# Two accumulator tiles of the last token group, moved to a pool of their own on the other side of SBUF

## The chip, the cores and the metric

The kernel runs on one core of one Trainium2 chip. Times are device microseconds (us) of one execution; of several runs the median is taken. An engine's name stands for its row in the profile: PE is the matrix engine, PEld its weight loads, DVE the vector engine, ACT the scalar engine, POOL the GpSimd engine (here it only issues DMAs), SP the engine that issues the other DMAs.

## The reference

Sigmoid attention for 8 batches of 12 heads, then a bilinear feed-forward net over all 3584 tokens:

```python
scores = scale * np.matmul(q, k.transpose(0, 1, 3, 2)) - np.log(S)   # S = 448, head size 64
attn = 1.0 / (1.0 + np.exp(-scores))
x = np.matmul(attn, v)          # heads side by side: 3584 tokens x 768
a = x @ w1                      # 768 -> 1024
b = x @ w2
h = a * b @ w3                  # 1024 -> 1024
out = h @ w_out                 # 1024 -> 768
```

All in float32; the weights come in as 64-bit words and are decoded on the chip.

## The kernel before

**Precision.** Each float32 operand is split into a high and a low part; a product is three matmuls (high by high, high by low, low by high).

**Stages.** Four token groups, each of two batches, go through attention (scores, sigmoid, times V) and then through `up(g)`, which computes `a`, `b` and their elementwise product. The two products of a 2 by 2 block split are made with seven block products instead of eight (L342 gives the operands, `POPS` and `NEEDS` the order of side work). A block product is 9 matmuls of 448 columns. The eight feature blocks `fc` take seven products each, so `up(g)` has 56 products. The last group, g = 3, is the "ending": nothing of attention is left to run beside it. After it come the product of `w3` with `w_out` (L852) and the final product with the activations (L984).

**Order.** From L577 on, the order of the instructions on all five engines is the order in which the code emits them. `take(stream, n)` advances a generator by n steps; nine steps of `up` are one block product. A load of `w` for the product five places ahead is issued on SP (L440, from L517) as each product begins; six `w` buffers go round.

**The last group's order** (L428 to L430) begins with `(fc, k)` = (0,0) (0,2) (1,0) (0,1) (1,2) (0,3) (0,4) (0,5) (0,6), and then (1,1) (2,0) (1,3) (1,4) (1,5) (1,6) (2,1) (2,2) (2,3) and so on. So `fc` 0 and 1 are interleaved, and two tiles of `fc` 1 are needed beside those of `fc` 0: `p_1` (the kept copy of product (1,0), read by the additions of (1,1) and (1,3)) and `c11_1` (the kept copy of (1,2), read by the multiplication of (1,6), L503). `kept` (L494 to L497) takes these two from the pool `p2`, all other kept tiles from `pm`.

**Pools in SBUF.** `pm` stands on the left side, open to the end of `phase_x` (L786). On the right side stand `pa` and `pf` (attention), and above them first `p1`, from step k = 46 on `p2` (the words `raw` and `f` of the last weights to be decoded, and the two tiles). After nine products of the ending the code does this:

```python
    take(filler, 9 * KH * 3 - 9)      # L740: the first nine products of the ending
    take(rest, 10 ** 6)
    phase_2.close()                   # p2
    phase_a.close()                   # pa, pf
    p3 = phase_w.enter_context(tc.tile_pool(name="p3", bufs=2, side="right"))   # L747
    load_wo(0); load_wo(1)            # L774, POOL: wof <- wo_dram
    load_w3(0, nc.gpsimd); load_w3(1, nc.gpsimd)
    for jc in range(NF):
        take(filler, 42 if jc else 54)                                          # L779
        split(woh[:, jc], wol[:, jc], wof.pop(jc), nc.scalar.copy, nc.vector)   # ACT L79, DVE L80
        load_wo(jc + 2)
```

`p3` takes the room that `pa`, `pf` and `p2` leave; its first instructions wait for the last use of what lay there. So at the point where POOL reaches the four loads of L774 to L777, six products of `fc` 1 and 2 that still use `p_1` and `c11_1` are not yet done; they are emitted by `take(filler, 54)`. The first split (ACT L79 into `woh`, DVE L80 into `wol`) stands, on ACT and on DVE, behind the instructions of these six products and ahead of those of (2,1).

`leave` (L502) multiplies into the output block and stores it to `g_dram` on POOL (L504).

Of the kernel before, what the change touches and what calls it, by code (L numbers as in the profile page):

```python
# [11 lines left out]
F32 = mybir.dt.float32  # L12
# [13 lines left out]
def sigmoid_attention_bilinear_ffn(  # L26
# [17 lines left out]
    B, H, D, S = qT.shape  # L44
    DM, DF = w1.shape[0], w1.shape[1] // 2
    NT = B * S
    P = 128
# [12 lines left out]
    def share_upper(kind):  # L60

        if upper:
            if upper[-1][0] == kind:
                return
            upper.pop()[1].close()
        if kind:
            stack = ExitStack()
            upper.append(
                (kind, stack, stack.enter_context(tc.tile_pool(name=kind, bufs=1, space=PSUM)))
            )  # L70
# [50 lines left out]
    phase_x = ExitStack()  # L121
# [90 lines left out]
    def attention(sp):  # L212
        a = pa.tile([P, 2, S], F32, name="a", bufs=4)
        sigmoid(a, sp)
        return a
# [220 lines left out]
    def load_weights(i):  # L436
        if i < len(stream):
            n = stream[i]
            ring[n] = pm.tile([P, 2, KH, P], F32R, name="w", bufs=RING)
            nc.sync.dma_start(out=ring[n].bitcast(F32), in_=w_dram[n % (NF * 7)])  # L440
# [33 lines left out]
    def up(g):  # L474

        at = {b: slice(b * S, (b + 1) * S) for b in (2 * g, 2 * g + 1)}
        ending = g == NG - 1
        parts = {fc: {} for fc in range(NF)}
        banks = {fc: {} for fc in range(NF)}

        def chain(fc, bank):
            if ending:
                tag = ("sp" if fc == 1 else "up0", "up1", "av", "av")[bank]
            else:
                tag = ("up0", "up1")[(len(banks[fc]) + fc) % 2]
            if tag == "sp":
                acc = ps.tile([P, 2, 512], F32, name="sp", bufs=2)[:, 0, :S]
            elif tag == "av":
                acc = ps.tile([P, 512], F32, name="up", tag=tag, bufs=2)[:, :S]
            else:  # L490
                acc = upper[-1][2].tile([P, 512], F32, name="up", tag=tag)[:, :S]
            banks[fc][bank] = acc

        def kept(name, fc=0):  # L494
            if ending and fc == 1:
                return p2[0].tile([P, S], F32, name=f"{name}_1", bufs=1)
            return pm.tile([P, S], F32, name=name, bufs=1)  # L497

        def add(out, a, b):
            nc.vector.tensor_tensor(out=out, in0=a, in1=b, op=ALU.add)  # L500

        def leave(fc, b, a, c, out):  # L502
            nc.vector.tensor_tensor(out=out, in0=a, in1=c, op=ALU.mult)  # L503
            nc.gpsimd.dma_start(out=g_dram[fc, :, at[b]], in_=out)  # L504

        first = stream[g * NF * 7:g * NF * 7 + 7]
        for done, n in enumerate(stream[g * NF * 7:(g + 1) * NF * 7]):
            share_upper("products")
            k = n % 7
            fc = n // 7 % NF  # L510
            name = PRODUCTS[k]
            part = parts[fc]
            if g == 0:
                while n not in ring:
                    next(weights)
            else:
                load_weights(place[n] + RING - 1)  # L517
            w = ring.pop(n)
            bank, start, stop = ((0, 1, 0), (1, 1, 0), (0, 0, 1), (1, 0, 1),
                                 (2, 1, 0), (3, 1, 1), (2, 0, 1))[k]  # L520
            if start:
                chain(fc, bank)
            a = banks[fc][bank]
            if ending:
                for other in NEEDS.get(done, ()):
                    change.need(other)
            elif fc == 0:
                for other in first[:done + (2, 4, 4)[g]]:
                    change.need(PRODUCTS[other % 7])
            for kc in range(KH):  # L530
                xh, xl = ops[g][name, kc]
                for m, (i, x) in enumerate(((0, xh), (0, xl), (1, xh))):
                    nc.tensor.matmul(  # L533
                        a, w[:, i, kc], x, start=bool(start) and kc == 0 and m == 0,
                        stop=bool(stop) and kc == KH - 1 and m == 2, skip_group_check=True,
                    )
                    if (kc, m) != (KH - 1, 2):
                        yield
            used.add(n)
            if k == 0:  # L540
                part["p"] = kept("p", fc)
                nc.scalar.copy(out=part["p"], in_=a)  # L542
            elif k == 1:
                part["u2"] = kept("u2")
                add(part["u2"], a, part["p"])
            elif k == 2:
                part["c11"] = kept("c11", fc)
                nc.scalar.copy(out=part["c11"], in_=a)
            elif k == 3:
                part["u3"] = kept("u3")  # L550
                add(part["u3"], a, part["p"])
            elif k == 4:
                part["c22"] = kept("c22")
                add(part["c22"], a, part["u3"])
            elif k == 5:
                u3 = part["u3"]
                add(u3, a, u3)
                leave(fc, 2 * g + 1, u3, part["c22"], u3)
            else:
                u2 = part["u2"]  # L560
                add(u2, a, u2)
                leave(fc, 2 * g, u2, part["c11"], kept("c22"))
            if not ending or done > 4:
                beside(g, n)
            yield

    def take(stream, n):
        done = 0
        for _ in itertools.islice(stream, n):
            done += 1  # L570
        return done
# [27 lines left out]
    starts = [sum(sizes[:k]) for k in range(NBURST + 1)]  # L599
    bursts = [items[i:i + n] for i, n in zip(starts, sizes)] + [[]]  # L600
    assert sum(sizes) == len(items)
    p2 = []

    def beside(g, n):

        if g == 0:
            take(change, 1)
            take(weights, 2)
        elif not take(change, 1):
            take(rest, 2)  # L610
# [73 lines left out]
    for k in range(NBURST + 1):  # L684
        if k == WINDOW[1]:
            phase_1.close()
            p2.append(phase_2.enter_context(tc.tile_pool(name="p2", bufs=2, side="right")))
            rest = prepare_rest()
        in_window = WINDOW[0] <= k < WINDOW[1]
        hi_cast = nc.scalar.copy if in_window or k in blocks else nc.vector.tensor_copy  # L690
        burst = bursts[k]
        for t, x in burst:
            prepare(t, x, hi_cast)
        if k < WINDOW[0]:
            if k == 1:
                next(weights)
            elif k > 1:
                take(change, 3)
                take(weights, 3 if k < 9 else 2 if k < 13 else 1)
        elif not in_window and k not in blocks and k < NBURST:  # L700
            take(change, 4 if k < 51 else 3)
        now = []
        for i, (t, x) in enumerate(short_at(burst, -1)):
            if x is None:
                sp = short_scores((qks.pop(2 * t), qks.pop(2 * t + 1)), i == 2)
            else:
                u, c = x
                if (k, i) == (0, 0):
                    high = low = None
                else:  # L710
                    high, low = splits[2 * t + u]
                sp = scores(high, low, c, i == 2, qks.get(2 * t + u))
            now.append((t, x, attention(sp)))
        if k == NBURST:
            take(change, 4)
            filler = up(NG - 1)
            take(filler, 9)
        by_place = {item[:2]: item for item in now}
        for item in previous:
            attend_item(*item)  # L720
        previous = [by_place[item] for item in short_at(burst, 0)]
        if k == WINDOW[0]:
            filler = up(0)
        if in_window:
            take(weights, 3 if k > WINDOW[0] + 1 else 0)
            done = k + 1 - WINDOW[0]
            if done % 2 == 0:
                upto, since = (GROUP * i // (WINDOW[1] - WINDOW[0]) for i in (done, done - 2))
                take(filler, upto - since)
            if k + 1 == WINDOW[1]:  # L730
                take(filler, 10)
                change = Units(1)
                take(weights, 10 ** 6)
                for n in range(RING - 1):
                    load_weights(NF * 7 + n)
        elif k in blocks:
            filler = up(blocks[k])
            take(filler, GROUP + 10)
            change = Units(blocks[k] + 1)
# [280 lines left out]
```

## Time and profile before

| | us |
|---|---|
| median of 3 runs | 976.32 |
| lowest, highest run | 973.87, 977.85 |
| the profiled execution | 974.72 |
| span of its trace | 972.9 |
| PE busy in the span | 959.7 (99%) |

The profiled execution is 1.8 us longer than the span of its trace and 1.6 us shorter than the median. The last group's `up` runs from about 581 to 696.6 us. An engine's busy time tells where work is; the chain of waits tells which work set the end; the timelines of single engines tell what stood behind what.

### The profile page before, as it was taken

Reading aid. Unit: us, or ns where it says so; the run is one execution under the profiler, and the core shown is the slowest. Engines: PE = TensorE matmul, PEld = TensorE weight load, DVE = VectorE, ACT = ScalarE, POOL = GpSimd, SP = SyncE. Lnnn points to the kernel's source line nnn. Section 1 sums busy time; section 2 is a strip of 40 time slices with the busy share of each in tenths; the row PEclk is TensorE's granted clock in tenths of the full one; section 3 lists DMA queues with packets and bytes.
Section 4 is the critical chain, followed back from the end, with each engine's and each line's share of the span. In section 5 each row is a group of like instructions: output and inputs, shape, how many; then the busy total and the mean of one; then the engine's idle time right before and its main releaser. Section 6 shows DMA issues by size and latency. Waiting matters only on the chain.

```text
span 972.9 us, 14115 instructions
## 1 busy us (share of the span) xinstructions
PE 959.7 (99%) x5236; PEld 757.5 (78%) x5236; DVE 657.7 (68%) x1060; ACT 400.2 (41%) x583; POOL 105.2 (11%) x182
## 2 busy tenths in 40 slices
PE   9999999999999999999999999799999999999998
PEld 4444666677665999958999648699999999999997
DVE  6869878987549788898887547344365657474643
ACT  7887556655557211282111572012043423232230
POOL 1110232222200111200121000211000000000000
PEclk9999999999999999999999999899999999999999
DMA  8764587776554999966999716888541034342402
GB/s 276 241 212 143 194 275 240 245 254 218 203 167 146 358 374 369 386 217 198 383 379 315 240 40 197 263 291 281 171 154 60 20 115 141 113 143 104 161 29 86
DMA packets 93781, 204.37 MB, mean 210 GB/s; under 512 B 9872, under 2 KB 57104, under 8 KB 93712
## 3 DMA queue, kind: packets, MB, share of 16 engines
q1 hardware_dynamic: 78432, 142.40, 44.3%
q0 software_dynamic: 15136, 60.83, 17.3%
q8 instruction: 42, 0.69, 0.3%
q10 hardware_dynamic: 144, 0.23, 0.1%
q14 instruction: 27, 0.22, 0.1%
HBM read 148.37 MB, written 55.05 MB: 209 GB/s over the span
## 4 chain that ended last, share of the span: by engine, by line
PE 95%; DVE 2%; ACT 1%; issue 1%; DMA 1%; DVEq 0%; ACTq 0%
PE up L533 42%; PE av L220 11%; PE sp L196 8%; PE av L984 7%; PE sp L984 7%; PE up L984 7%; PE sp L852 3%; PE av L852 3%; PE av L228 2%; PE third L196 1%; PE sp L207 1%; PE third L207 1%; DMA wof<-wo_dram 1%; ACT a L177 0%; DVE low L80 0%
## 5 line engine op out<-in xcount | busy, mean ns | idle before, releaser
L533 PE MATMUL up<-hS,w 128*128 128x448 f32 x702 | 217.3, 370 | 6.1 <-DVE u L500 6.1
L533 PE MATMUL up<-hA,w 128*128 128x448 f32 x510 | 160.1, 368 | 0.3 <-ACT a L177 0.3
L533 PEld LDWEIGHTS up<-hS,w 128*128 128x128 f32 x702 | 133.1, 190 | 22.6 <-DVE u L500 6.5
L177 ACT ACTIVATE a<-sp,bias 128x896 f32<-128x896 f32 x132 | 129.9, 1011 | 49.4 <-PE sp L196 24.5
L533 PE MATMUL up<-lS,w 128*128 128x448 f32 x351 | 129.4, 369 | 0.0
L220 PE MATMUL av<-a,vv 128*64 128x448 f32 x576 | 122.8, 551 | 0.0
L533 PEld LDWEIGHTS up<-hA,w 128*128 128x128 f32 x510 | 95.8, 188 | 13.9 <-issue 4.4
L533 PE MATMUL up<-lA,w 128*128 128x448 f32 x255 | 93.4, 366 | 0.0
L220 PEld LDWEIGHTS av<-a,vv 128*64 128x64 f32 x576 | 35.5, 136 | 67.7 <-issue 67.3
L542 ACT COPY p<-up 128x448 f32<-128x448 f32 x31 | 16.6, 534 | 154.6 <-PE up L533 135.5
L500 DVE TENSOR_TENSOR u<-up,p 128x448 f32<-128x448 f32 x64 | 39.9, 623 | 58.0 <-PE up L533 53.8
L533 PEld LDWEIGHTS up<-lS,w 128*128 128x128 f32 x351 | 66.7, 190 | 5.7
L984 PE MATMUL av<-gh,wo 128*128 128x448 f32 x224 | 68.6, 367 | 0.0
L984 PE MATMUL sp<-gh,wo 128*128 128x448 f32 x224 | 68.5, 367 | 0.0
L984 PE MATMUL up<-gh,wo 128*128 128x448 f32 x224 | 68.5, 367 | 0.0
L500 DVE TENSOR_TENSOR u<-up,u 128x448 f32<-128x448 f32 x64 | 39.8, 622 | 34.0 <-PE up L533 33.7
L79 ACT CAST gh<-gf 128x896 fp32r<-128x896 f32 x40 | 35.7, 943 | 56.2 <-PE sp L984 50.0
L80 DVE TENSOR_TENSOR gl<-gf,gh 128x896 fp32r<-128x896 f32 x40 | 41.9, 1087 | 23.7 <-ACT gh L79 23.7
L80 DVE TENSOR_TENSOR low<-qk,high 128x896 fp32r<-128x896 f32 x47 | 51.3, 1091 | 7.4 <-ACT high L79 6.3
L196 PEld LDWEIGHTS sp<-high 64*128 64x128 f32 x232 | 21.8, 184 | 42.8 <-ACT a L177 31.0
L89 ACT ACTIVATE f<-raw 128x768 f32<-128x768 f32 (+2 forms) x48 | 34.5, 718 | 48.4 <-DMA w_dram<-f 11.5
L533 PEld LDWEIGHTS up<-lA,w 128*128 128x128 f32 x255 | 47.9, 188 | 4.1
(145 smaller groups left out, 1745.9 us busy)
## 6 DMA issues: line engine op xcount, KB each, us to landing
w<-w_dram SPq DMA_DIRECT2D x168, 384.0 KB, 5.4
gf<-g_dram SPq DMA_DIRECT2D x16, 896.0 KB, 5.4
w_dram<-w POOLq DMA_DIRECT2D x36, 384.0 KB, 4.6
raw<-w POOLq DMA_DIRECT2D x16, 768.0 KB, 6.6
qk<-qT SPq DMA_DIRECT2D x48, 224.0 KB, 4.8
qk<-kT SPq DMA_DIRECT2D x47, 224.0 KB, 5.1
out<-o_sb SPq DMA_DIRECT2D x47, 224.0 KB, 1.9
vv<-vL SPq DMA_DIRECT2D x24, 384.0 KB, 3.5
```

Source lines behind the costliest of these rows:

```text
L79: hi_engine(out=dst_hi, in_=src)
L80: lo_engine.tensor_tensor(out=dst_lo, in0=src, in1=dst_hi, op=ALU.subtract)
L89: nc.scalar.activation(f, raw[..., 1].bitcast(F32), AF.Abs, scale=HW_SCALE)
L177: nc.scalar.activation(dst, src, AF.Sigmoid, bias=bias[:n], scale=scale)
L196: nc.tensor.matmul(sp[:, j], k[rows, 1, at:at + P], q[rows, 0], start=m == 0, stop=m == len(terms) - 1,)
L207: nc.tensor.matmul(sp[HEADS[u], j], qk[rows, 1, FULL:], qk[rows, 0], start=True, stop=True)
L220: nc.tensor.matmul(acc[cols, :S], vv[:, c, at:at + D], a[:, j], start=start, stop=stop,)
L228: nc.tensor.matmul(acc[cols, :S], vs[HEADS[u], cols], a[HEADS[u], j], start=ends[u][0], stop=ends[u][1],)
L500: nc.vector.tensor_tensor(out=out, in0=a, in1=b, op=ALU.add)
L533: nc.tensor.matmul(a, w[:, i, kc], x, start=bool(start) and kc == 0 and m == 0, stop=bool(stop) and kc == KH - 1 and m == 2, skip_group_ch ...
L852: nc.tensor.matmul(acc, a[:, jc], w[:, jc, ms], start=(jc == 0 and m == 0), stop=(jc == NF - 1 and m == 2),)
L984: nc.tensor.matmul(acc, w[:, fc, ms], g[:, fc], start=start and fc == 0 and m == 0, stop=fc == NH - 1 and m == 2, skip_group_check=True,)
```

## The change

The two tiles come from a new pool `px`, opened on the left side at step k = 46, just ahead of `p2`, and closed with `phase_x`. They keep their size and their users. `p2` no longer holds them.

```diff
         def kept(name, fc=0):
             if ending and fc == 1:
-                return p2[0].tile([P, S], F32, name=f"{name}_1", bufs=1)
+                return px[0].tile([P, S], F32, name=f"{name}_1", bufs=1)
             return pm.tile([P, S], F32, name=name, bufs=1)
...
-    p2 = []
+    p2, px = [], []
...
         if k == WINDOW[1]:
             phase_1.close()
+            px.append(phase_x.enter_context(tc.tile_pool(name="px", bufs=1, side="left")))
             p2.append(phase_2.enter_context(tc.tile_pool(name="p2", bufs=2, side="right")))
             rest = prepare_rest()
```

## Rows read from the trace of the kernel before

**Rows 1.** Page, parts 1 and 2: busy time; PE's clock in 40 slices.
```profile
PE 959.7 (99%) x5236; PEld 757.5 (78%) x5236; DVE 657.7 (68%) x1060; ACT 400.2 (41%) x583; POOL 105.2 (11%) x182
...
PEclk9999999999999999999999999899999999999999
```

**Rows 2.** Chain of waits, 520 to 700 us: start, duration, what.
```profile
593.62 18.25 PE up L533 x90
...
613.65 5.40 DMA wof<-wo_dram
...
620.06 0.96 DVE wol L80
621.02 0.55 DVE u L500
621.56 0.04 issue
621.61 75.02 PE up L533 x351
```

**Rows 3.** Timeline of POOL: start, duration, instruction, [idle before, releaser].
```profile
532.68 0.54 POOL L469 DMA_DIRECT2D wo_dram<-f  x1
...
602.64 0.54 POOL L504 DMA_DIRECT2D g_dram<-c  x1 [1.29 <-DVE c L503]
613.65 1.09 POOL L772 DMA_DIRECT2D wof<-wo_dram  x2 [10.47 <-DVE c L503]
614.74 1.07 POOL L758 DMA_DIRECT2D w<-w_dram  x2
615.83 0.55 POOL L504 DMA_DIRECT2D g_dram<-u  x1
```

**Rows 4.** Timeline of ACT, and of DVE behind it, around the first split.
```profile
619.19 0.83 ACT L79 CAST woh<-wof 128x768 fp32r<-128x768 f32 x1 [14.06 <-DMA wof<-wo_dram]
...
594.74 1.69 DVE L246 TENSOR_TENSOR lS<-A,hS 128x448 fp32r<-128x448 f32 x3
...
610.73 0.63 DVE L503 TENSOR_TENSOR u<-u,c 128x448 f32<-128x448 f32 x1
...
612.62 0.62 DVE L503 TENSOR_TENSOR c<-u,c 128x448 f32<-128x448 f32 x1
...
625.49 0.62 DVE L500 TENSOR_TENSOR u<-up,p 128x448 f32<-128x448 f32 x1 [3.94 <-DMA g_dram<-u]
```

**Rows 5.** Timeline of PE: the last matmul before it stands still.
```profile
615.13 0.37 PE L533 MATMUL up<-hA,w 128*128 128x448 f32 x1
```

**Rows 6.** Busy time by stretch, with count, granted clock, DMA share, GB/s.
```profile
615.30:621.60 6.30, 0.20 (x1) 0.00 (x0) 1.49 (x2) 2.06 (x3) 1.79 (x4) 0.86 0.96 311
621.60:626.60 5.00, 4.99 (x13) 4.51 (x14) 0.62 (x1) 0.00 (x0) 0.37 (x1) 0.50 0.82 306
626.60:696.60 70.00, 70.00 (x340) 63.58 (x339) 32.12 (x47) 11.64 (x18) 8.28 (x16) 1.00 0.80 254
...
619.00:620.00 1.00, 0.00 (x0) 0.00 (x0) 0.00 (x0) 0.81 (x2) 0.00 (x0) 0.89 0.96 367
```

**Rows 7.** Timeline of PEld at a hiccup; two long stretches of `up` matmuls.
```profile
340.96 0.19 PEld L533 LDWEIGHTS up<-hA,w 128*128 128x128 f32 x1 [0.17 <-issue]
...
442.90:541.00 98.10, 98.10 (x486) 90.93 (x485) 76.48 (x149) 17.71 (x33) 16.14 (x29) 1.00 0.95 336
341.30:410.00 68.70, 68.70 (x334) 62.40 (x333) 55.97 (x110) 12.71 (x23) 12.71 (x23) 1.00 1.01 374
```

**Rows 8.** SP's `w` loads issued at 608.2, 613.7, 615.5 us: count, size, landing.
```profile
w<-w_dram SPq DMA_DIRECT2D x1, 384.0 KB, 3.7
...
w<-w_dram SPq DMA_DIRECT2D x1, 384.0 KB, 6.4
...
w<-w_dram SPq DMA_DIRECT2D x1, 384.0 KB, 8.1
```

**Rows 9.** POOL's store issued at 615.8 us, its landing; stretch of the burst.
```profile
g_dram<-u POOLq DMA_DIRECT2D x1, 224.0 KB, 9.6
...
617.00:625.00 8.00, 3.39 (x9) 3.08 (x10) 1.49 (x2) 2.06 (x3) 0.54 (x1) 0.67 0.99 351
```

## The prediction

> **What bounds the kernel now.** I read the page first: PE is busy for 959.7 of 972.9 us, and its clock is down in one slice of 40 only, the one around 620 us [rows 1]. So PE sets the time nearly everywhere, and what can be won lies where it stands still. The chain of waits is next, for the stretch of the last group. It runs on PE throughout, except from 611.9 to 621.6 us, where it leaves PE for DVE, then for the landing of `wof` (5.40 us), the split, and the addition `u` at 621.02, after which PE goes on [rows 2]. The third view is POOL's timeline: POOL is free after the store of 602.64, but its next instruction, the first `wof` load, starts at 613.65, after 10.47 us of waiting for DVE's multiplication `c` L503 [rows 3]. That multiplication is the one of product (1,6), the last reader of `c11_1`. The timelines of ACT and DVE close the ring: ACT waits 14.06 us for that load; DVE is done with the multiplication at 613.24 (612.62 and 0.62), and its next instruction in order is the split into `wol`, at 620.06 [rows 2, 4]. Behind it, in DVE's order, stands the addition of product (2,1). PE's product (2,3) goes on in the bank that this addition reads, and cannot start before it. PE's last matmul before that begins at 615.13 [rows 5].
>
> So the wait is one for room. `p3` lies where `p2` lay, `p2` holds `c11_1`, and DVE frees that only at 613.24.
>
> **What the change removes.** The two tiles leave `p2`, so nothing under `p3` is read by the six products any more. What else lay there is old by 602.64: the last decoded words were stored at 532.68 [rows 3], and the attention tiles of `pf` were last read by DVE's subtractions from 594.74 to 596.43 [rows 4]. POOL therefore reaches the first load right behind the store of 602.64, at 603.2, which is 10.5 us earlier. With the same 5.40 us to land it is there at 608.6, and ACT, idle then, has split it by 609.5. DVE reaches `wol` at 613.24 and finds its input ready: 0.96 us, to 614.20, then the addition of (2,1), 0.55 to 0.62 us, to 614.8. PE wants that bank at 615.13 + 0.20 = 615.33. It is on time by 0.5 us, and the wait on the landing has 613.24 − 0.84 − 608.6 = 3.8 us to spare.
>
> **The sum.** (a) PE stands still from 615.33 to 621.61: 6.28 us. (b) The 351 matmuls of the 39 products behind it take 75.02 us. At the pace ahead of the stop, 18.25 us for 90 or 0.2028 us each [rows 2], they would take 71.17: 3.85 us more are lost. Two things are in this. From 621.6 to 626.6 the granted clock is 0.50, the 1.2 GHz level, after it fell near 620, with PE idle since 615.5 [rows 6]; of the 351, 12 fall in there (351 less the 339 weight loads of the stretch behind), 4.99 us where 2.43 would do: 2.56 us. The other 339 take 70.0 us at full clock, 0.2065 each, where 68.75 would do: 1.25 us [rows 6]. With no stop, (a) and the clock's part certainly go. The 1.25 go too if PE keeps the pace that it had. That two paces exist at full clock is seen elsewhere: 485 weight loads in 98.10 us (0.2023) and 333 in 68.70 (0.2063), and the slower stretch begins at a hiccup of 0.17 us [rows 7]. I take it that an interruption starts the slow pace. Sum: 6.28 + 3.85 = 10.1 us. The profiled execution of 974.72 becomes 964.6. It lay 1.6 under the median, and 976.32 becomes 966.2.
>
> **What it adds or moves.** The tiles' copies and readers stay as they are, with the same durations. `px` opens over room of `p1`, whose users ended some 250 us before the first write: nothing. The pools that follow on the left wait for `pm` to the end of the stage anyway; `px`, done by 613.24, adds nothing. What moves on POOL is four loads, two of 384 KB and two of 512 KB, or 1.835 MB, from 613.65 to 603.2. No POOL instruction stands between: the stores of (1,5) and (1,6) come behind, and with POOL no longer held they go out at about 611.8 and 613.6 instead of 615.83 and 616.4. The burst now falls on a PE at full speed, which draws a `w` load of 0.393 MB every 9 × 0.2028 = 1.83 us, or 215 GB/s.
>
> **Do those loads come late?** A load issued as one product begins is wanted five products later, 9.1 us, less some 0.4 for issue and early weight loading: 8.7 us. Alone it lands in 3.7, amid the burst in 6.4 and 8.1 [rows 8]. Worked out as one common line at the 351 GB/s of the burst [rows 9]: 1.2 loads outstanding, the burst's 1.835 MB, and the loads of 604.6 and 606.4, less what 3.2 us serve, is 0.47 + 1.84 + 0.79 − 1.12 = 1.97 MB, 5.6 us, and with some 2.5 us fixed (3.7 less 1.1 for its own bytes) 8.1 us, an estimate. The next ones gain 0.7 us each. Bounds: 6.4 (none late) and 9.6, the longest landing of the stretch [rows 9], which is 0.9 us late. I take 8.1, no wait, since its own row says the same.
>
> The rows show loads that wait behind what POOL issued ahead of them, 8.1 us against 3.7. The Trainium skill, DMA: Bandwidth & Descriptors, section "Queues, rings and completion order", has each DMA engine take turns between the queue rows it has work for. By that alone SP would keep half of 351 GB/s, fall 40 GB/s short for some 10.5 us and land in under 6 us, so that no load could be late and that rival's chance would be nil; the load with 8.1 us speaks against leaning on it.
>
> **The other queue.** The addition of (2,3) rewrites the tile that the store of (1,5) reads, and before it waited 3.94 us for that, since the store went out behind the burst and took 9.6 us [rows 4, 9]. Now it goes out at 611.8, when the common line is down to 1.3 MB: landed by 618. The addition is ready at 617.2; PE needs its result through that of (2,4) at 620.8, so DVE may start it as late as 619.4. Covered by 1.4 us.
>
> **The rivals.**
> - *The slow pace stays.* Any small hiccup from 603 on starts it, as at 340.96. Against: 442.9 to 541 us, at a DMA share of 0.95, kept the fast one [rows 7]. For: the burst. It gives back 1.25: 967.5.
> - *A load or the store is late.* Up to 0.9 us for `w` (9.6 against 8.7), or 2.0 for the store (9.6 against 7.6), each with the slow pace: 966.2 + 0.9 + 1.25 = 968.4, or 969.5.
> - *The change does not do what it says.* If POOL waits for another tile that `p3` covers, until much the same time: 976.3. Against: no user of that room after 596.43 but the two tiles.
> - *Slower.* The place is products (2,3) to (3,0), the mechanism the burst of POOL ahead of SP's loads. Lateness costs PE one for one, and an idle time as long as the one of before takes the clock with it. To end slower, a load must be later than 10.1 − 3.8 = 6.3 us, a landing of 15 us; slower by 0.5% needs 20 and gives 981. The longest row is 9.6.
>
> **How the numbers follow.** Forecast 966.2, chance 0.58. Slow pace 967.5, 0.22. Something late 968.4 to 969.5, 0.12. No effect 976.3, 0.06. Slower 981, 0.02. The range starts at the lowest run less the sum, 973.87 − 10.1 = 963.8, and ends at 970.0, behind the late cases; 0.08 is left out by cases, some more by scatter. This kernel's runs tell 0.5% from no change, 4.9 us: faster 0.92, same 0.06, slower 0.02.
>
> **What would show it.** Right: POOL's first `wof` load near 603, the split into `wol` near 613.3 behind `c` with no idle time, PE with no stop at 615 and its clock at 1.00 through 600 to 640, and 39 products in 71.2 us from 615.3 on. Half right: 0.2065 us a matmul in that stretch. Wrong: POOL still held to 613; a `w` landing beyond 8.7 us with idle PE weight loads at 613 to 621; DVE idle at 617 to 620 on the store of `u` with PE idle behind it.

## The result, and the profile after

| | before | after |
|---|---|---|
| median | 976.19 us (7 runs) | 967.06 us (7 runs) |
| lowest, highest | 973.87, 977.85 | 964.20, 971.66 |
| profiled execution | 974.72 | 964.66 |
| span of its trace | 972.9 | 962.9 |

Ratio after to before 0.9909, 95% interval 0.9883 to 0.9935. A second comparison of the same two kernels (E9 below) gave 0.9905, 0.989 to 0.992. The change makes the kernel about 9 us faster; the profiled execution is 10.1 us shorter.

The page after shows PE's clock with no dent (compare [rows 1]):

```profile
PEclk9999999999999999999999999999999999999999
```

The chain of waits of 520 to 700 us no longer leaves PE. All 459 matmuls from product (0,3) on follow each other, 93.03 / 459 = 0.2027 us each; in [rows 2] the chain left PE after the first 90:

```profile
593.55 93.03 PE up L533 x459
686.58 4.16 PE sp L853 x24
```

POOL's timeline, the lines that answer to [rows 3]. The first load stands at 603.62, behind the store of 602.57, and the two stores of (1,5) and (1,6) go out as soon as DVE has their data:

```profile
602.57 0.54 POOL L504 DMA_DIRECT2D g_dram<-c  x1 [1.29 <-DVE c L503]
603.62 1.09 POOL L773 DMA_DIRECT2D wof<-wo_dram  x2 [0.51 <-issue]
604.70 1.07 POOL L759 DMA_DIRECT2D w<-w_dram  x2
611.69 0.55 POOL L504 DMA_DIRECT2D g_dram<-u  x1 [5.92 <-DVE u L503]
613.59 0.55 POOL L504 DMA_DIRECT2D g_dram<-c  x1 [1.34 <-DVE c L503]
```

ACT's timeline, for [rows 4]: the split waits 5.09 us for the load, not 14.06, and is over before DVE needs it.

```profile
610.16 0.83 ACT L79 CAST woh<-wof 128x768 fp32r<-128x768 f32 x1 [5.09 <-DMA wof<-wo_dram]
```

DVE's timeline, for [rows 4]. The split into `wol` at 613.10 follows the multiplication of 612.56 with no idle time; the additions of (2,3) and (2,4), at 617.61 and 619.67, each wait for a store:

```profile
612.56 0.63 DVE L503 TENSOR_TENSOR c<-u,c 128x448 f32<-128x448 f32 x1
613.10 0.95 DVE L80 TENSOR_TENSOR wol<-wof,woh 128x768 fp32r<-128x768 f32 x1
613.97 0.62 DVE L500 TENSOR_TENSOR u<-up,p 128x448 f32<-128x448 f32 x1
617.61 0.62 DVE L500 TENSOR_TENSOR u<-up,p 128x448 f32<-128x448 f32 x1 [3.02 <-DMA g_dram<-u]
619.67 0.62 DVE L500 TENSOR_TENSOR c<-up,u 128x448 f32<-128x448 f32 x1 [1.43 <-DMA g_dram<-c]
```

SP's `w` loads issued at 606.4 and in 611.5 to 613 us, for [rows 8]: 8.2 and 7.9 us to land.

```profile
w<-w_dram SPq DMA_DIRECT2D x1, 384.0 KB, 8.2
...
w<-w_dram SPq DMA_DIRECT2D x1, 384.0 KB, 7.9
```

### The profile page after: what moved, and what is told of

Same layout as the page of the kernel before. It is cut to its first block, busy times and chain, and to the rows that moved or that the text cites. A ratio compares the mean times of both kernels' runs of the same rounds, so it can differ in the third digit from the quotient of the medians.

```text
span 962.9 us, 14120 instructions
## 1 busy us (share of the span) xinstructions
PE 955.6 (99%) x5236; PEld 756.4 (79%) x5236; DVE 657.1 (68%) x1060; ACT 400.2 (42%) x583; POOL 104.8 (11%) x182
## 4 chain that ended last, share of the span: by engine, by line
PE 95%; DVE 2%; DMA 1%; ACT 1%; issue 1%; SPq 0%; DVEq 0%; ACTq 0%
PE up L533 42%; PE av L220 11%; PE sp L196 8%; PE av L985 7%; PE sp L985 7%; PE up L985 7%; PE av L853 3%; PE sp L853 3%; PE av L228 2%; PE third L196 1%; PE sp L207 1%; DMA vv<-vL 1%; PE third L207 1%; ACT a L177 0%; DVE low L80 0%
## 5 line engine op out<-in xcount | busy, mean ns | idle before, releaser
L533 PE MATMUL up<-hS,w 128*128 128x448 f32 x702 | 214.6, 366 | 0.0
L548 ACT COPY c<-up 128x448 f32<-128x448 f32 x31 | 16.6, 534 | 85.7 <-PE up L533 60.0
```

Source lines behind the costliest of these rows:

```text
L533: nc.tensor.matmul(a, w[:, i, kc], x, start=bool(start) and kc == 0 and m == 0, stop=bool(stop) and kc == KH - 1 and m == 2, skip_group_ch ...
```

## The experiments

All traces are compared over one stretch: from the end of product (1,2), where (0,3) begins, to the first matmul of the `w3` by `w_out` product. It is 459 matmuls in each kernel: 103.0 us before, 93.0 after. "Lost at stops" is worked out from PE's timeline: the time from the start of the last matmul before a stop to the start of the next, less one matmul; the first matmul behind a stop is a little longer than the others, which counts to the rest.

| kernel | stretch | lost at stops | the rest over 93.0 | clock fell |
|---|---|---|---|---|
| before | 103.0 | 6.3 | 3.7 | yes |
| after | 93.0 | 0 | 0 | no |
| E1 only `p_1` moved | 102.7 | 7.0 | 2.6 | yes |
| E2 only `c11_1` moved | 94.9 | 1.7 | 0.2 | no |
| E3 split later | 103.5 | 7.3 | 3.2 | yes |
| E4 loads later | 93.0 | 0 | 0 | no |
| E5 stop of 1.5 us | 95.0 | 1.9 | 0.1 | no |
| E6 stop of 6.4 us | 104.8 | 7.8 | 4.0 | yes |
| E7 two loads more | 96.2 | 2.7 | 0.4 | no |
| E8 four loads more | 104.0 | 6.9 | 4.0 | yes |
| E9 the change again | 93.6 | 0.3 | 0.3 | no |
| E10 as E4 | 93.0 | 0 | 0 | no |

**E1 and E2: which tile holds the room.** The changed kernel with one of the two tiles put back into `p2` (E2: `"c11"` in place of `"p"`; the edit adds a line, so L503 of the rows of before is L504 here):

```diff
-                return px[0].tile([P, S], F32, name=f"{name}_1", bufs=1)
+                pool = px[0] if name == "p" else p2[0]
+                return pool.tile([P, S], F32, name=f"{name}_1", bufs=1)
```

> Only p_1 goes to the new pool; c11_1 stays in p2, under p3. Theory (the loads wait for the last reader of what lies under p3, and that is c11_1, read at 612.6): nothing is won. POOL's first wof load stays at 613.6, PE stops for 6.3 us at product (2,3), the clock falls, and the stretch from product (1,1) region (593.6 us) to the start of the w3 by w_out product lasts 103.0 us as before. Rival (p_1, with two of the three readings, holds the room, or any lighter p2 is enough): the stop goes and the stretch lasts 93.0 us.

> Only c11_1 goes to the new pool; p_1 stays in p2, its last reader is the addition of (1,3), 606.4 to 607.0 us. Theory: the loads start at 607.4, the first lands after 5.4 to 7.5 us, at 612.8 to 614.9, the split into wol ends at 614.6 to 616.7, the addition of (2,1) at 615.2 to 617.3, and PE, which wants it at 615.3, stops for 0 to 2 us. Its clock stays up. If an interruption starts the slow pace, the 39 products behind take 72.4 us instead of 71.2; stretch 93.0 to 96.3 us. Rival (only c11_1 counts): loads at 603.6, stretch 93.0 us.

E1 took 974.78 us beside 975.09 of before: nothing won. POOL's timeline is as in [rows 3], with the same wait for the multiplication of (1,6):

```profile
614.06 1.09 POOL L774 DMA_DIRECT2D wof<-wo_dram  x2 [10.47 <-DVE c L504]
```

And of the waits (total, times, longest), PE's own shows the stop:

```profile
PE up L534 <- DVE u L501: 6.8, 1, 6.8
```

Its stop is 0.7 us longer than that of before because its first load landed in 6.1 us instead of 5.4.

E2 took 968.40 us. Its trace runs 1.9 us late from before the stretch on, so its times compare with after's plus 1.9. The loads started at 609.49, 0.65 us behind the addition of (1,3), the last reader of `p_1`. POOL's timeline:

```profile
609.49 1.09 POOL L774 DMA_DIRECT2D wof<-wo_dram  x2 [4.52 <-DMA w<-w_dram]
```

The profile names a `w` load as what ended this wait, and not the addition. By its time the addition fits: in before the loads started 0.41 us behind the last reader. What held the last 0.25 us here is not shown.

DVE's timeline, the additions of (1,3), (2,3) and (2,4):

```profile
608.22 0.62 DVE L501 TENSOR_TENSOR u<-up,p 128x448 f32<-128x448 f32 x1 [3.02 <-PE up L534]
...
622.77 0.62 DVE L501 TENSOR_TENSOR u<-up,p 128x448 f32<-128x448 f32 x1 [5.28 <-DMA g_dram<-u]
623.71 0.62 DVE L501 TENSOR_TENSOR c<-up,u 128x448 f32<-128x448 f32 x1 [0.31 <-DMA g_dram<-c]
```

PE's waits:

```profile
PE up L534 <- DVE c L501: 1.1, 1, 1.1
PE up L534 <- DVE u L501: 0.2, 1, 0.2
```

So the loads wait for the later of the two tiles' last readers: with `c11_1` left in `p2` they start as in before, with `p_1` left they start where its last reader ends. E2's small loss has two parts. The first is 0.2 us of waiting for the split, within its expectation (start to start, 0.4 us). The second, 1.1 us (start to start, 1.3), was not in it: the stores of (1,5) and (1,6), closer behind the burst, land late, so the addition of (2,3) waits 5.28 us for the one and that of (2,4) 0.31 us more for the other.

**E3: the split alone out of the way.** The kernel before with

```diff
-        take(filler, 42 if jc else 54)
+        take(filler, 42 if jc else 96)
```

> The kernel before, tiles in p2, loads emitted where they were; only the first split into woh and wol is emitted 42 steps later (and all later splits with it). POOL is still held to 613.6. Theory of one wait (only the split ahead of the addition of (2,1) stops PE): the stop goes, stretch 93.0 us. Theory of a queue (POOL, held by the loads, also holds the store of (1,5), which then goes out at 615.8 behind the burst and lands at 625): PE passes 615.3, but the addition of (2,3) waits for that store until 625, and PE stops at product (2,6), at 620.8, for some 5.5 us; clock down again for some us; stretch 99 to 103 us.

It took 976.40 us beside 975.09: no gain at all. PE passed (2,3), and stopped at (2,6) instead. POOL's timeline, the held loads and the store of (1,5) behind them:

```profile
614.80 1.09 POOL L772 DMA_DIRECT2D wof<-wo_dram  x2 [10.47 <-DVE c L503]
...
616.98 0.55 POOL L504 DMA_DIRECT2D g_dram<-u  x1
```

DVE's timeline, the additions of (2,3) and (2,4):

```profile
627.60 0.62 DVE L500 TENSOR_TENSOR u<-up,p 128x448 f32<-128x448 f32 x1 [12.05 <-DMA g_dram<-u]
628.61 0.62 DVE L500 TENSOR_TENSOR c<-up,u 128x448 f32<-128x448 f32 x1 [0.39 <-DMA g_dram<-c]
```

PE's waits, the stop by the addition of (2,4):

```profile
PE up L533 <- DVE c L500: 7.2, 1, 7.2
```

The store of (1,5) waited on POOL behind the held loads, then landed behind their bytes, 10.5 us after it went out. The stop of 7.3 us is longer than the 5.5 expected, in part because that landing was longer than the 9.6 of [rows 9], in part because the addition of (2,4) then waited 0.39 us for the store of (1,6), which the expectation had left out. Behind the stop that the chain showed lay a second one of much the same size: the chain of waits alone, which named the split, would have led to an edit that wins nothing.

**E4 and E10: the same gain with no new pool.** The kernel before, the loads emitted behind the six products:

```diff
+    take(filler, 54)
     load_wo(0)
     load_wo(1)
     load_w3(0, nc.gpsimd)
     load_w3(1, nc.gpsimd)
     for jc in range(NF):
-        take(filler, 42 if jc else 54)
+        take(filler, 42)
```

> The kernel before, tiles in p2; the four loads are emitted behind the six products (and so behind their stores on POOL), and the splits 42 steps later than before. No pool is added. Theory: the wait for c11_1 is over when POOL comes to the loads, at 613.6 to 614, the stores of (1,5) and (1,6) go out at 611.7 and 613.5, nothing in DVE's order needs the loads until 623, and PE doesn't stop: stretch 93.0 to 93.5 us, time as with the change. Rival (the pools' side is what counts, through addresses or the load of the DMA queues): PE still stops, stretch over 96 us.

> The kernel before with only the four loads emitted behind the six products (and the splits 42 steps later), in five rounds. Theory (the whole gain is the removed wait of POOL, by whatever means): the same time as the changed kernel within 0.3%, ratio to before 0.987 to 0.993. Rival (the new place of the tiles or of p2 has a gain of its own): at least 0.4% slower than the changed kernel.

> The changed kernel again, in five rounds beside the kernel before. Forecast by the sum: 10.1 us less than before (ratio 0.9897), with single runs scattered over some 4 us, since the slow pace comes and goes in stretches of up to 1.3 us each.

E4 took 964.54 us. Its stretch is after's to the hundredth, as its chain of waits shows:

```profile
593.44 93.03 PE up L533 x459
```

POOL's timeline has the loads at 614.43, behind both stores:

```profile
613.47 0.54 POOL L504 DMA_DIRECT2D g_dram<-c  x1 [1.35 <-DMA w<-w_dram]
614.43 1.09 POOL L772 DMA_DIRECT2D wof<-wo_dram  x2 [0.42 <-issue]
```

Timed on the same chip beside each other: E10 965.77 us, ratio to before 0.9907 (0.989 to 0.9923); the change (E9) 965.52 us, 0.9905 (0.989 to 0.992). The two can't be told apart. The side of SBUF has no worth of its own. Nor has the early start of the loads: in E4 they start at 614.43, later than in before, and land just as late. What cost time was what stood behind POOL's wait: the stores on POOL, and the split on DVE ahead of the addition of (2,1). E3 and E4 differ in the place of the loads alone, and their stretches are 103.5 and 93.0 us. E9's trace, of another execution of the changed kernel, shows in addition a weight load that came late, in its chain of waits:

```profile
609.19 9.39 DMA w<-w_dram
618.62 69.58 PE up L533 x342
```

And among PE's waits:

```profile
PE up L533 <- DMA w<-w_dram: 0.2, 1, 0.2
```

A landing of 9.39 us made PE stand still for 0.3, so that one was wanted some 9.1 us after issue. In E7 (below) a landing of 9.1 us cost 0.3, so there it was 8.8. The change, with 8.2 us in its profiled execution, runs close to this limit.

**E5 and E6: what a stop costs by itself.** The changed kernel with n = 4 or 13 additions on a tile of zeros that nobody reads, on DVE ahead of the addition of (2,1); no transfer is moved:

```diff
+            spare = px[0].tile([P, S], F32, name="spare")
+            nc.vector.memset(spare, 0.0)
...
+                for _ in range(n if ending and done == 15 else 0):
+                    add(spare, spare, spare)
                 add(part["u2"], a, part["p"])
```

> The changed kernel with four idle additions (128x448, about 0.55 us each in a row) on DVE ahead of the addition of product (2,1); no transfer is moved. The addition then ends near 616.8 us where PE wants it at 615.3: PE stops for 1.5 us. Clock stays at full. Theory A (any interruption of PE starts the slow pace of 0.2066 us a matmul): stretch from 593.6 us to the w3 by w_out product 93.0 + 1.5 + 1.25 = 95.8 us. Theory B (an interruption costs its own length and no more, as long as the clock stays up): 94.5 us.

> The changed kernel with thirteen such additions, 7.1 us: PE stops for 6.4 us at product (2,3), with no burst and no waiting store at that time. Theory (the 3.8 us that the kernel before lost behind its stop belong to the stop, through the clock and the pace, not to the transfers): the clock falls near 620 us and comes back some 5 us after PE goes on; stretch 93.0 + 6.4 + 2.6 = 102.0 us at the fast pace, 103.3 at the slow one. Rival (the transfers that piled up beside the stop cost the 3.8 us): clock falls, but the stretch is under 100.5 us.

The additions took 0.65 us each, not 0.55, so the stops were 1.9 and 7.8 us. E5, 967.63 us: by the chain of waits the 351 matmuls from the restart on took 71.41 us, 0.2034 each, the fast pace.

```profile
618.14 71.41 PE up L533 x351
```

E6, 976.78 us: in its chain the same 351 took 75.26 us, much as in [rows 2].

```profile
623.41 75.26 PE up L533 x351
```

Its clock fell while PE stood still, as the stretch of 618 to 619 us shows (busy times by engine, granted clock 0.86, DMA share, GB/s). At the restart, in 623 to 624, the clock is at 0.50 and the DMA engines move nothing (0 GB/s):

```profile
618.00:619.00 1.00, 0.00 (x0) 0.00 (x0) 0.93 (x3) 0.00 (x0) 0.00 (x0) 0.86 1.05 429
...
623.00:624.00 1.00, 0.59 (x2) 0.55 (x3) 0.36 (x1) 0.00 (x0) 0.00 (x0) 0.50 0.00 0
```

So a short stop costs its own length (theory B), and the long one 4.0 us more, lost behind a restart with no transfer beside it: the transfers are not their cause. By PE's timeline 2.6 of the 4.0 fall on the 15 matmuls behind the restart, at the low clock, and 1.3 on the slow pace of the others. E1, behind a stop of 7.0 us, lost the same 2.6 at the low clock and then ran at the fast pace: the price of such a stop is the clock's part, and the slow pace need not follow it.

**E7 and E8: how much more the queue bears.** The changed kernel with n = 2 or 4 loads of 512 KB behind the four:

```diff
     load_w3(1, nc.gpsimd)
+    for i in range(n):
+        more = px[0].tile([P, NF, P], F32, name=f"more{i}")
+        nc.gpsimd.dma_start(out=more, in_=w3_dram[i])
```

> The changed kernel with two more 512 KB loads on POOL right behind the four (their tiles are read by nobody). Theory of a common line (w loads wait behind what POOL issued ahead of them): with 1.05 MB more at 351 GB/s the w loads land in up to 8.2 + 3.0 = 11.2 us where 8.7 is allowed; PE waits for weights by 2 to 2.5 us in all between 614 and 625, the store of (1,5) lands after 8.8 us; clock stays up; stretch 95 to 96 us. Rival (the DMA engines take turns between SP's and POOL's queues, so POOL's backlog hardly delays w): w lands within 8.7 us, stretch 93.0 to 93.5 us.

> The same with four more 512 KB loads, 2.1 MB. Common line: w loads land in up to 14 us, PE waits 5 to 6 us in all, spread over several products, and the store of (1,5) lands after 11 to 12 us, so the addition of (2,3) waits too; stretch 98 to 101 us, more if the clock falls. Rival (turns): as with two more, stretch under 94 us for PE's weights, and only POOL's own store is late (11 to 12 us, 4 us over what is allowed): 97 us.

E7, 968.13 us. The waits of PE and PEld:

```profile
PE up L533 <- DVE c L500: 1.8, 1, 1.8
...
PEld up L533 <- DMA w<-w_dram: 1.0, 2, 0.5
```

The landing of a `w` load issued in 613 to 614 us, and of the store of (1,5):

```profile
w<-w_dram SPq DMA_DIRECT2D x1, 384.0 KB, 10.5
...
g_dram<-u POOLq DMA_DIRECT2D x1, 224.0 KB, 10.3
```

And the stretch of 613 to 622 us, where the DMA engines have no room left (share 1.03, 411 GB/s, above the 351 of [rows 9]):

```profile
613.00:622.00 9.00, 8.69 (x40) 7.08 (x39) 1.93 (x3) 1.27 (x2) 1.09 (x2) 1.00 1.03 411
```

E8, 976.03 us, no better than before (974.03 on that chip). The third and fourth of the added loads started only at 609.36 and 610.54. The same waits:

```profile
PE up L533 <- DVE c L500: 6.5, 1, 6.5
...
PEld up L533 <- DMA w<-w_dram: 0.5, 1, 0.5
```

And the landing of the store of (1,5):

```profile
g_dram<-u POOLq DMA_DIRECT2D x1, 224.0 KB, 14.3
```

Loads of `w` do wait behind POOL's bytes: the common line said up to 11.2 us with two loads more, 10.5 was measured, and turns alone would have kept them under 8.7. But with four more they came to 11.2, not 14, while the store in POOL's own queue took 14.3. Neither rule holds alone. What PE lost was mostly not weights (0.8 and 0.3 us) but the additions of (2,3) and (2,4), held by stores (1.9 and 6.6 us).

## Why the prediction held, and where its steps were off

**What held.** The stop goes whole (6.28 us), the 3.85 us behind it too: the stretch is 10.0 us shorter where the sum said 10.1. The median came to 967.06 where 966.2 was forecast. That the profiled execution came to 964.66, where the sum said 964.6, is in part luck: single runs lie between 964.20 and 971.66, and this one is near the lowest. The reason was the one given: in E1 and E2 the loads start by the last reader of whatever tile is left under `p3`, and E4 gets the whole gain with the tiles where they were. POOL's first load was forecast for 603.2 and stood at 603.62, the split into `wol` for 613.24 (613.10), the addition of (2,1) done by 614.8 (614.59).

**The first load's landing was undersized.** 5.40 us were taken over from before. The load issued at 603.62 took 6.4 to land, and it started 0.4 us later than forecast:

```profile
wof<-wo_dram POOLq DMA_DIRECT2D x1, 384.0 KB, 6.4
```

ACT split at 610.16 in place of 608.6. Of the 3.8 us to spare, 2.1 were left (613.10 less 610.99). One row had been taken for a fixed price. In the other runs the first load landed in 4.9 us (E4) to 6.9 us (E7); in E1, where it stands as in before, it took 6.1, and beside a PE at full speed 5.4 in E2 and 4.9 in E4. So the running PE alone does not set it; what does is open.

**The weight loads: the peak was right, the recovery was not.** Forecast 8.1 us at most, measured 8.2. But the loads behind it were to gain 0.7 us each, and still took 7.9 at 612. The step left out what POOL issues behind the burst (two stores and the third `wof`), and the measured burst is no pure common line, as E7 and E8 show. The allowed 8.7 us were nearly right: 8.8 by E7, 9.1 by E9. The rival "a load is late" did happen in E9's profiled execution, for 0.3 us instead of 0.9.

**A wait was missed.** The addition of (2,4) writes the tile that the store of (1,6) reads. I had listed the store of (1,5) and the addition of (2,3) alone, covered by 1.4 us. That cover held: the addition of (2,3) began at 617.61. The other is tighter: the addition of (2,4) began at 619.67, after 1.43 us of waiting for the store, and was done at 620.29, where PE's (2,6) wants it at 620.7. Some 0.4 us were to spare, and the text gave no price for it. With E2's burst, later by 4 us against the products, the two waits already cost 1.1 us.

**The place of the "slower" rival was wrong.** It put the danger into SP's weight loads and the deciding point at a landing of 15 us. E8 gets there by POOL's own queue, with weights that land in 11.2 us at most: a store of 14.3 us holds DVE, DVE holds PE for 6.6 us, the clock falls, and the kernel is as slow as before. Two megabytes more on POOL were enough.

**The slow pace.** "I take it that an interruption starts the slow pace" falls. E2, E5 and E7 interrupt PE by 0.2 to 1.9 us at full clock and go on at the fast one. The very hiccup that the prediction read in [rows 7] stands in the trace after too, and the fast pace goes on behind it (timeline of PEld in after, then the busy times of the stretch that showed 334 matmuls in before):

```profile
342.25 0.19 PEld L533 LDWEIGHTS up<-hA,w 128*128 128x128 f32 x1 [0.17 <-issue]
...
341.30:410.00 68.70, 68.70 (x340) 63.52 (x339) 56.67 (x112) 13.24 (x24) 13.57 (x25) 1.00 1.01 379
```

Where the clock fell, the slow pace followed in four kernels of five. Two rows of the same 50 us (634 to 684), E1 and E6, both behind a fall, show 249 and 243 matmuls. E1:

```profile
634.00:684.00 50.00, 50.00 (x249) 46.35 (x248) 21.68 (x34) 10.56 (x16) 6.16 (x12) 1.00 0.89 287
```

E6:

```profile
634.00:684.00 50.00, 50.00 (x243) 45.41 (x243) 21.24 (x33) 10.54 (x16) 5.99 (x11) 1.00 0.89 285
```

The term of 1.25 us was sized rightly for the execution shown, yet it is not the price of a stop: E1 stopped longer and lost 2.6 us behind the stop where before lost 3.7. The change did not turn that stretch of 341 to 410 us fast: in E7 and E8, which run the changed kernel's instructions there, it shows 333 and 334 matmuls. Why the pace changes is open. Its coming and going may be a part of the scatter of single runs, 964.2 to 971.7 us; no run separates that.

## What to carry to other kernels

A pool that opens where another lay waits for the last reader of everything under it, so two small tiles can hold up the loads of a whole stage, and with them all that stands behind on the same queue. Ask of each long-lived tile which pool's end it delays; either put it elsewhere or emit the loads behind its last reader, which here gave the same. And follow the queue past the wait that the chain names: with the split moved alone, the held store was next and cost as much.

## What the runs showed that was not expected

- At full granted clock the 128x448 matmuls run at one of two paces, 0.2028 or 0.2066 us each, and keep one for tens of microseconds. The changes come behind stops, but also with no wait in the trace: in E5 the slow pace began near 491 us with no step between two matmuls above 0.207 us.
- Stops of 6.3 to 7.8 us (five kernels) cost 2.6 to 4.0 us more than their length: 1.9 to 2.7 us at the low clock (0.50 for some microseconds after the restart), and in four of the five 1.2 to 1.3 us by the slow pace. Stops of up to 1.9 us cost at most 0.4 us beyond theirs.
- A 224 KB store that lands in 4.4 us beside weight loads alone (before) took 10.3 us behind 2.9 MB of loads on its own queue (E7), and 14.3 us behind 3.9 MB (E8). A 384 KB load on SP's queue beside them went from 3.7 to 10.5 and 11.2 us.
